# Block 0 of a fused attention and SwiGLU kernel: the norm ahead of the weights' rounding, v from a second queue, and block 1's loads held back

## The chip, the cores and the metric

The kernel runs on one core of a Trainium2 chip. A core has a matrix engine (TensorE, PE in the profile, with its weight loads shown apart as PEld), a vector engine (VectorE, DVE), a scalar engine (ScalarE, ACT), GpSimd (POOL) and SyncE (SP), which here only issues transfers. Each engine carries out its instructions in the order in which they stand in its queue; a wait of one instruction holds all behind it. Transfers are carried out by 16 DMA engines, whichever engine issued them.

The metric is the device time of one launch in microseconds. Before the change the median of four runs is 1042.65 us (1041.47 to 1042.95).

## The reference: what is computed

There are 8 sequences of 576 tokens with 8 heads of width 64, and a feed-forward block over the 4608 tokens.

```
kv  = k^T v                              per sequence and head, 64 x 64
o   = q kv                               per token and head
x   = o / sqrt(mean(o*o) + 1e-6) * g     the norm, over the 64 columns of a head
g   = x @ w_gate ;  val = x @ w_val      4608 x 512  by  512 x 1536
out = (silu(g) * val) @ w_out            4608 x 1536 by 1536 x 512
```

All is float32. The weights come as float64 and are read as pairs of 32-bit words, from which the kernel makes float32 values on the chip ("rounding" below).

## The kernel before

The 4608 tokens are worked in nine blocks of 512 (`NB = 9`). A block's x is 512 tokens by 512 columns. Blocks 1 to 8 use products of the Strassen and Winograd kind (seven products for eight, in classes `Up`, `Inner` and `Down`). Block 0 is different: its up projection is plain (`plain_up`, `plain_end`), because in this stretch the weights arrive and are still being rounded.

**Attention of a block** (class `Att`). `load_kv` and `load_q` issue the loads from SP (L228, L267). `kv` multiplies k and v (L285) into two PSUM tiles, which ACT copies and DVE adds (L291, L292). `turn_q` transposes q on PE (L306) and copies the result to SBUF, on ACT (L308) or on DVE (L310). `product` multiplies by kv (L326), ACT squares the result (L337) and DVE sums the squares (L338). `root` is a chain of eleven small DVE instructions (L344 to L356). `scale` applies the root (two multiplications through the helper of L113). `turn_x` transposes the normed x on PE (L373), and ACT copies it with the gain (L374). Each of these works on half a block (two of four token tiles); `half` is product, root and scale of one half.

**Rounding of a weight piece** (class `Words`). A piece is 128 x 512 values, 512 KB as float64 words. It is loaded by SP (L135) into one of four buffers of the pool `ld`, which the q tiles and later k and v use too. `round_to` makes two ACT instructions (L144, L146) and four DVE instructions (L147, L152, L153, L157) of it. There are 36 pieces: 12 of w_gate and w_val in turn (`g0, v0, g1, v1, ...`), then 12 of w_out. `weights(upto)` rounds pieces up to a number, and before each one issues loads up to four pieces ahead.

**Block 0 in program order.** q of half 0, k and v, q of half 1 are loaded; `weights(1)` loads four pieces and rounds one; `first` does the attention up to the transposed x of half 0; `weights(2)`; `plain_up` for f = 0 and half 0 of the tokens; `second` does root, scale and turn of half 1; then, for each of the twelve f, `weights(2 * (f + 2))` and `plain_up` (L953: four matmuls with the gate, four with the value weights; ACT's silu, L958; DVE's product, L113, which writes h). For f = 0 and 1 the two halves of the tokens are done separately. Then come the w_out pieces' rest, sums for the down projection, block 1's loads, and `plain_end`. A scheduler of the framework sets the order on each engine; it can move instructions past each other where nothing forbids it. `tc.issue_after(ins)` puts the instructions of its block behind `ins` in the order of the engine that `ins` runs on, without a wait of other engines.

Block 1's k and v of the first heads go into a tile of their own (`xi`), its q into tiles of the pool `t`, and the k and v of the other heads into `ld`.

Of the kernel before, what the change touches and what calls it, by code (L numbers as in the profile page):

```python
# [12 lines left out]
ACT = mybir.ActivationFunctionType  # L13
# [5 lines left out]
def kernel(  # L19
# [41 lines left out]
    nc = tc.nc  # L61
# [11 lines left out]
    NP = NF // 2  # L73
# [20 lines left out]
    a_psum = pool("a_psum", 1, space=PS)  # L94
    b_psum = pool("b_psum", 3, space=PS)
# [23 lines left out]
    class Words:  # L119
# [12 lines left out]
        def __init__(self, src, shape):  # L132
            self.raw = ld_pool.tile([P, LD], U32, name="ld")[:, 0 : 2 * BLK]
            dst = self.raw.rearrange("p (a b) -> p a b", a=shape[0])
            nc.sync.dma_start(out=dst, in_=src)  # L135
            self.shape = shape

        def round_to(self, dst):
# [30 lines left out]
    words = {}  # L169

    def load_w(name, j):
        src = wviews[name][1]
        if name == "o":
            words[name, j] = Words(src[:, j : j + 1, :], (1,))
        else:
            words[name, j] = Words(src[:, :, 2 * P * j : 2 * P * (j + 1)], (NS,))
# [8 lines left out]
    class Att:  # L185
# [29 lines left out]
        def load_kv(self, g):  # L215


            if self.n == B:
                return
            for i, (views, src) in enumerate(((self.k, k), (self.v, v))):  # L220
                tile_ = self.place_kv(g, i)
                for e in range(2):
                    j, s0 = 2 * g + e, 0
                    for r in range(2):
                        m = KT - (r != e)
                        at = 2 * D * (KT - r) * e
                        t = tile_[r * D : (r + 1) * D, at : at + 2 * D * m].rearrange("p (h x) -> p h x", h=2)
                        nc.sync.dma_start(  # L228
                            out=t,
                            in_=src[self.n, 2 * j : 2 * j + 2, s0 : s0 + m * D].rearrange("h (p t) d -> p h (t d)", t=m),  # L230
                        )
                        views[j, r] = t.rearrange("p h (t d) -> p h t d", t=m)
                        s0 += m * D
# [60 lines left out]
        def turn_q(self, i, pools=None):  # L294

            if i == 0:
                self.qt = ring().rearrange("p j (t c) -> p t j c", t=T)
            if self.n >= TURNED:
                to = self.qt[:, :, 2 * i : 2 * i + 2].rearrange("p t j c -> p j t c")
                nc.vector.transpose(out=to.rearrange("p j t c -> p (j t c)"), in_=self.q[i])  # L300
                return
            for t in (2 * i, 2 * i + 1):
                pool = pools[t % 2] if pools else m_psum
                ps = pool.tile([P, NS, P], F32, name=pool.name[0])
                for j in range(NS):
                    nc.tensor.transpose(ps[:, j], self.q[t][:, j], ident)  # L306
                if t % 2 or self.n == 1 or self.n > DEEP:
                    nc.scalar.copy(out=self.qt[:, t], in_=ps)  # L308
                else:
                    nc.vector.tensor_copy(out=self.qt[:, t], in_=ps)  # L310

        def product(self, i, pools=None):

            pools = pools or (m_psum, m_psum)
            self.ps[i] = [pool.tile([P, 2, NS, D], F32, name=pool.name[0]) for pool in pools]
            for t in range(2):  # L320
                for j in range(NS):
                    for b, _, p0, p1 in self.parts(2 * i + t):
                        for p in range(p0, p1, D):
                            for u in range(2):
                                rows = slice(u * D, (u + 1) * D)
                                nc.tensor.matmul(  # L326
                                    self.ps[i][u][p : p + D, t, j, :],
                                    lhsT=self.qt[rows, 2 * i + t, j, p : p + D], rhs=kvs[b % 3][rows, j, :],
                                    start=True, stop=True,
                                )  # L330
            if self.z is None or 0 < self.n < TURNED:
                self.z = st_pool.tile([P, 2, 2, 2, NS], F32, name="z")
            if i == 0:
                self.sq = ring().rearrange("p f (t j d) -> p f t j d", t=2, j=NS)
            for u in range(2):
                sq = self.sq[:, 2 * i + u]
                nc.scalar.activation(out=sq, in_=self.ps[i][u], func=ACT.Square)  # L337
                nc.vector.tensor_reduce(out=self.z[:, i, u], in_=sq, axis=mybir.AxisListType.X, op=OP.add)  # L338

        def root(self, i, k=1):  # L340
# [24 lines left out]
        def turn_x(self, i):  # L365
            if i == 0:
                self.x = x_pool.tile([P, 7, 2, HB], F32, name="x")
            xt = self.xts[:, i].rearrange("p t j u d -> p t j (u d)")
            for j in range(0, NS, 2):
                ps = m_psum.tile([P, 2, 2, P], F32, name="m")  # L370
                for e in range(2):
                    for t in range(2):
                        nc.tensor.transpose(ps[:, e, t], xt[:, t, j + e], ident)  # L373
                nc.scalar.activation(  # L374
                    out=self.x[:, 2 * i + j // 2], in_=ps.rearrange("p e t c -> p e (t c)"), func=ACT.Copy, scale=gain
                )

# [49 lines left out]
        def first(self):  # L427
            self.turn_q(0, (b_psum, c_psum))
            for g in range(2):
                self.kv(g)  # L430
            self.half(0)
            self.turn_q(1, (b_psum, c_psum))
            self.product(1, (b_psum, a_psum))
            self.turn_x(0)
            return self.scaled

        def second(self):
            self.root(1)
# [46 lines left out]
    DEEP = 2  # L485
# [482 lines left out]

    pieces = [(x, j) for j in range(NF) for x in "gv"] + [("o", j) for j in range(NF)]
    loaded = rounded = 0  # L970

    def weights(upto):
        nonlocal loaded, rounded
        while rounded < min(upto, len(pieces)):
            while loaded < min(rounded + 4, len(pieces)):
                load_w(*pieces[loaded])
                loaded += 1
            round_w(*pieces[rounded])
            rounded += 1

# [8 lines left out]
    for g in range(2):  # L989
        blocks[0].load_kv(g)  # L990
    blocks[0].load_q(1)
    weights(1)
    scaled = blocks[0].first()

    for n in range(NB):
        ffn = Ffn(n, blocks[n])
        nxt = blocks[n + 1] if n + 1 < NB else None
        if n == 0:

            with tc.issue_after(scaled.ins):  # L1000
                weights(2)
            ffn.plain_up(0, (0,))
            scaled = blocks[0].second()
            for f in range(NF):
                with tc.issue_after(scaled.ins):
                    weights(2 * (f + 2))
                if f == 1:
                    ffn.plain_up(1, (0,))
                    ffn.plain_up(0, (1,))
                ffn.plain_up(f, (1,)) if f == 1 else ffn.plain_up(f) if f else None  # L1010
            weights(len(pieces))
            pairs = wo.rearrange("p (j e) d -> p e j d", e=2)
            t2(pairs[:, 0, :, HD:DM], pairs[:, 1, :, HD:DM], pairs[:, 0, :, 0:HD])
            nxt.room = x_pool.tile([P, 3, 7, P], F32, name="xi").rearrange("p a b c -> p (a b c)")
            for i in range(2):
                nxt.load_kv(i)
            for i in range(2):
                nxt.load_q(i)
            ffn.plain_end()
            for g in range(2):  # L1020
                nxt.kv(g)
        else:

            def third():
                nxt.kv(0)
                nxt.load_kv(1)

            def two_thirds():
                nxt.kv(1)
                if nxt.n < TURNED:  # L1030
                    for i in range(2):
                        nxt.load_q(i)

            ffn.up({4: third, 8: two_thirds} if nxt else {})
        if nxt:
            nxt.turn()
        if n + 2 < NB:
            blocks[n + 2].load_kv(0)
        if TURNED - 2 <= n < NB - 2:
            ffn.loads = blocks[n + 2].load_q  # L1040
            if n >= DEEP:
                for i in range(2):
                    ffn.loads(i)
        ffn.down(nxt)
        if n == 0:

            with tc.issue_after(nxt.halves[0].ins):
                for j in range(NP):
                    t2(wv[j][:, 0:2], wv[j][:, 2:4], wg[j][:, 0:2])
# [31 lines left out]
```

## Time and profile before

| what | value |
|---|---|
| median of the runs | 1042.65 us |
| the profiled execution's own time | 1042.89 us |
| its span | 1041.1 us |
| first matmul of block 0's up projection (L953) | 33.05 us |
| start of f = 1 in it | 39.37 us |
| end of it (start of block 1's L285) | 118.40 us |
| DMA engines' busy share, 2 to 14 us | 0.97 |

Times in the profile are microseconds from the span's start. A row of the timeline gives start, length, engine, line, operation and shapes, and in brackets the idle time of the engine before it and what ended it. The chain that ended last is followed back from the end of the program: at each step it names what released an instruction. The granted clock is the share of full speed that the chip let TensorE run at. In the profile each matmul of 32-bit numbers appears as two instructions, so that the four matmuls of a line are shown as x8.

The rest of the profile is shown in the prediction.

### The profile page before, as it was taken

What the parts mean: (1) busy time and instruction counts of PE and PEld (TensorE: products, weight loads), DVE (VectorE), ACT (ScalarE), POOL (GpSimd) and SP (SyncE); (2) the same over time, 40 slices, a digit from 0 to 9 for tenths busy, and PEclk for the clock granted to TensorE, in tenths of its full rate; (3) what the DMA queues carried; (4) which work ended last, traced back from release to release, by engine and by line L of the source; (5) the groups of instructions that cost most, each with busy time, mean ns of one, the idle gap of its engine ahead of it and who ended that gap; (6) DMA issues with size and microseconds to landing.
All of it is one profiled execution on the core that took longest, in us unless ns stands there. A gap on an engine that the chain in (4) does not pass through costs nothing.

```text
span 1041.1 us, 21533 instructions
## 1 busy us (share of the span) xinstructions
PE 1014.8 (97%) x8588; PEld 911.1 (88%) x8588; DVE 703.1 (68%) x1203; ACT 230.9 (22%) x356; POOL 369.1 (35%) x280
## 2 busy tenths in 40 slices
PE   5899999999999999999999999999999999999998
PEld 4644688788899989998999899988999899989997
DVE  1999596889655756666666756683668566856661
ACT  1666211122212121111121121211222121212110
POOL 0000433445024631563056305550355126512670
PEclk9899999999999999999999999999999999999999
DMA  8797303766467546764677377826862666166611
GB/s 232 217 275 245 115 1 105 195 181 162 111 192 233 149 88 201 249 170 70 197 242 198 55 203 230 223 44 169 249 194 58 156 207 191 30 152 209 192 31 41
DMA packets 255043, 168.15 MB, mean 162 GB/s; under 512 B 124640, under 2 KB 230240, under 8 KB 254944
## 3 DMA queue, kind: packets, MB, share of 16 engines
q1 hardware_dynamic: 229536, 163.63, 56.0%
q10 hardware_dynamic: 25344, 3.15, 1.9%
q8 instruction: 68, 1.11, 0.4%
q14 instruction: 31, 0.25, 0.1%
q0 software_dynamic: 64, 0.00, 0.0%
HBM read 138.02 MB, written 22.41 MB: 154 GB/s over the span
## 4 chain that ended last, share of the span: by engine, by line
PE 91%; DVE 4%; DMA 1%; SPq 1%; issue 1%; POOL 0%; ACT 0%; DVEq 0%; POOLq 0%; ACTq 0%
PE b L659 25%; PE b L510 20%; PE c L659 12%; PE c L510 10%; PE a L659 6%; PE a L510 5%; PE b L953 4%; PE c L953 4%; PE m L285 2%; PE m L326 1%; SPq L228 1%; DMA ld<-in_moe_w_gate_dram 1%; DVE xi L112 1%; DVE r L112 1%; PE m L373 1%
## 5 line engine op out<-in xcount | busy, mean ns | idle before, releaser
L111 POOL TENSOR_TENSOR r<-r 128x256 f32<-128x256 f32 (+1 forms) x105 | 110.8, 1061 | 308.8 <-DVE r L111 234.5
L111 DVE TENSOR_TENSOR r<-b,r 128x512 f32<-128x512 f32 (+1 forms) x273 | 161.9, 605 | 63.7 <-PE b L659 59.2
L112 POOL TENSOR_TENSOR t<-wo 128x512 f32<-128x512 f32 x81 | 115.6, 1452 | 197.6 <-DVE wo L111 109.2
L111 DVE TENSOR_TENSOR r<-c,r 128x512 f32<-128x512 f32 (+1 forms) x179 | 108.3, 617 | 89.5 <-PE c L659 49.3
L659 PE MATMUL b<-x,t 128*128 128x128 f32 x1092 | 151.0, 275 | 0.0
L659 PEld LDWEIGHTS b<-x,t 128*128 128x128 f32 x1092 | 136.5, 192 | 0.6
L111 DVE TENSOR_TENSOR r<-a,r 128x512 f32<-128x512 f32 (+1 forms) x99 | 62.4, 630 | 110.2 <-PE a L510 65.9
L113 POOL TENSOR_TENSOR h<-r 128x1024 f32<-128x1024 f32 (+1 forms) x40 | 81.5, 2052 | 87.5 <-DVE r L111 73.8
L659 PE MATMUL c<-xi,t 128*128 128x128 f32 x840 | 112.2, 275 | 0.3 <-DVE xi L111 0.3
L659 PEld LDWEIGHTS c<-xi,t 128*128 128x128 f32 x840 | 102.8, 192 | 0.4 <-DVE xi L111 0.4
L510 PE MATMUL b<-wo,h 128*128 128x256 f32 x432 | 99.4, 382 | 0.1
L510 PE MATMUL b<-t,h 128*128 128x256 f32 x432 | 96.9, 381 | 0.0
L510 PEld LDWEIGHTS b<-t,h 128*128 128x128 f32 x432 | 81.3, 190 | 11.3 <-issue 0.2
L510 PEld LDWEIGHTS b<-wo,h 128*128 128x128 f32 x432 | 79.9, 190 | 12.7 <-DVE h L113 2.5
L673 ACT COPY r<-b 128x512 f32<-128x512 f32 x63 | 36.9, 585 | 212.7 <-PE b L659 212.7
L659 PE MATMUL b<-xi,t 128*128 128x128 f32 x588 | 79.7, 276 | 0.0
L659 PEld LDWEIGHTS b<-xi,t 128*128 128x128 f32 x588 | 72.4, 192 | 0.0
L659 PE MATMUL b<-x,wg 128*128 128x128 f32 x336 | 52.7, 279 | 0.2 <-DVE x L112 0.2
L659 PE MATMUL b<-x,wv 128*128 128x128 f32 x336 | 51.3, 275 | 0.0
L510 PE MATMUL c<-t,s 128*128 128x256 f32 x216 | 48.3, 380 | 0.0
L510 PE MATMUL a<-wo,h 128*128 128x256 f32 x216 | 48.3, 379 | 0.0
L510 PE MATMUL c<-wo,h 128*128 128x256 f32 x216 | 48.1, 379 | 0.0
(131 smaller groups left out, 1590.1 us busy)
## 6 DMA issues: line engine op xcount, KB each, us to landing
t<-w SPq DMA_DIRECT2D x336, 256.0 KB, 3.4
out_dram<-r SPq DMA_DIRECT2D x17, 512.0 KB, 3.1
ld<-in_moe_w_gate_dram SPq DMA_DIRECT2D x12, 512.0 KB, 5.0
ld<-in_moe_w_val_dram SPq DMA_DIRECT2D x12, 512.0 KB, 4.9
ld<-in_moe_w_out_dram SPq DMA_DIRECT2D x12, 512.0 KB, 4.7
w<-t SPq DMA_DIRECT2D x18, 256.0 KB, 2.5
w<-xi SPq DMA_DIRECT2D x12, 384.0 KB, 3.0
ld<-in_k_dram SPq DMA_DIRECT2D x26, 160.0 KB, 3.7
```

What stands on the lines that cost most here:

```text
L111: add = lambda e, o, a, b: e.tensor_tensor(out=o, in0=a, in1=b, op=OP.add)
L112: sub = lambda e, o, a, b: e.tensor_tensor(out=o, in0=a, in1=b, op=OP.subtract)
L113: mul = lambda e, o, a, b: e.tensor_tensor(out=o, in0=a, in1=b, op=OP.mult)
L228: nc.sync.dma_start(out=t, in_=src[self.n, 2 * j : 2 * j + 2, s0 : s0 + m * D].rearrange("h (p t) d -> p h (t d)", t=m),)
L285: nc.tensor.matmul(self.kv_ps[r][u * D : (u + 1) * D, j, :], lhsT=self.k[j, r][:, u, c, :], rhs=self.v[j, r][:, u, c, :], start=(c == 0), ...
L326: nc.tensor.matmul(self.ps[i][u][p : p + D, t, j, :], lhsT=self.qt[rows, 2 * i + t, j, p : p + D], rhs=kvs[b % 3][rows, j, :], start=True, ...
L373: nc.tensor.transpose(ps[:, e, t], xt[:, t, j + e], ident)
L510: nc.tensor.matmul(banks[e][:, e], lhsT=lhsT, rhs=rhs, start=first and i == 0 and (e == 0 or banks[0] is not banks[1]), stop=i == self.ste ...
L659: nc.tensor.matmul(ps[:, i, f], lhsT=self.weight(o, p, f), rhs=self.operand(o, p), start=first and (i, f) == (0, 0), stop=True, skip_group ...
L673: nc.scalar.copy(out=dst, in_=ps)
L953: nc.tensor.matmul(t, lhsT=w[f // 2][:, i, P * (f % 2) : P * (f % 2 + 1)], rhs=x[:, i, of], start=(i == 0), stop=(i == NS - 1),)
```

## The change

There are five edits.

1. `load_kv` issues block 0's v (eight transfers) from ScalarE's queue instead of SP's.
2. Loading and rounding of weights are split: `load_weights(4)` issues the first four loads, and nothing is rounded before `first`. The first two pieces are rounded behind the last square of half 0 (on ACT) and behind the scale of half 0 (on DVE). From f = 1 on, rounding also stands behind the last copy of x on ACT.
3. In `first`, `product` of half 1 stands inside `issue_after(self.scaled.ins)`: on DVE its sums come behind the scale of half 0.
4. `turn_q` copies on DVE only the first of the four tiles, in every block; before, it was every other tile in blocks 0 and 2 and none in block 1.
5. The thirteen transfers of block 1's q and of its k and v into `xi`, and those of its other k and v, stand on SP's queue behind the load of the 30th of the 36 pieces.

```diff
@@ class Words
-            nc.sync.dma_start(out=dst, in_=src)
+            self.sent = nc.sync.dma_start(out=dst, in_=src)
@@ load_kv
-                        nc.sync.dma_start(
+                        queue = nc.scalar if self.n == 0 and i else nc.sync
+                        queue.dma_start(
@@ turn_q
-                if t % 2 or self.n == 1 or self.n > DEEP:
+                if t:
                     nc.scalar.copy(out=self.qt[:, t], in_=ps)
                 else:
                     nc.vector.tensor_copy(out=self.qt[:, t], in_=ps)
@@ product
-                nc.scalar.activation(out=sq, in_=self.ps[i][u], func=ACT.Square)
+                self.squared = nc.scalar.activation(out=sq, in_=self.ps[i][u], func=ACT.Square)
@@ turn_x
-                nc.scalar.activation(
+                self.copied = nc.scalar.activation(
@@ first
             self.half(0)
+            squared = self.squared
             self.turn_q(1, (b_psum, c_psum))
-            self.product(1, (b_psum, a_psum))
+            with tc.issue_after(self.scaled.ins):
+                self.product(1, (b_psum, a_psum))
             self.turn_x(0)
-            return self.scaled
+            return squared, self.scaled
@@ weights
+    sent = None
+
+    def load_weights(upto):
+        nonlocal loaded, sent
+        while loaded < min(upto, len(pieces)):
+            load_w(*pieces[loaded])
+            loaded += 1
+            if loaded == len(pieces) - NP:
+                sent = words[pieces[loaded - 1]].sent
+
     def weights(upto):
-        nonlocal loaded, rounded
+        nonlocal rounded
         while rounded < min(upto, len(pieces)):
-            while loaded < min(rounded + 4, len(pieces)):
-                load_w(*pieces[loaded])
-                loaded += 1
+            load_weights(rounded + 4)
             round_w(*pieces[rounded])
             rounded += 1
@@ block 0
-    weights(1)
-    scaled = blocks[0].first()
+    load_weights(4)
+    squared, scaled = blocks[0].first()
...
-            with tc.issue_after(scaled.ins):
+            with tc.issue_after(squared.ins), tc.issue_after(scaled.ins):
                 weights(2)
             ffn.plain_up(0, (0,))
             scaled = blocks[0].second()
             for f in range(NF):
-                with tc.issue_after(scaled.ins):
+                with tc.issue_after(scaled.ins), tc.issue_after(blocks[0].copied.ins) if f else ExitStack():
                     weights(2 * (f + 2))
...
-            for i in range(2):
-                nxt.load_kv(i)
-            for i in range(2):
-                nxt.load_q(i)
+            with tc.issue_after(sent.ins):
+                for i in range(2):
+                    nxt.load_kv(i)
+                for i in range(2):
+                    nxt.load_q(i)
```

## The prediction

> **What bounds the kernel now.** I read the busy shares first, then the chain that ended last over the first 66 us, then the windows with the granted clock, then DVE, ACT and SP in order of time. The page says who is the bound:
>
> ```profile
> PE 1014.8 (97%) x8588; PEld 911.1 (88%) x8588; DVE 703.1 (68%) x1203; ACT 230.9 (22%) x356; POOL 369.1 (35%) x280
> ```
>
> PE is idle 26 us of 1041.1, nearly all of it before block 0's first projection and around 200 to 245 us. The change touches the first of these. The chain there (start, length, what):
>
> ```profile
> 13.14 0.58 SPq L267
> ...
> 13.76 7.51 DMA ld<-in_moe_w_gate_dram
> ...
> 21.29 0.43 DVE r L152
> 21.72 0.61 DVE r L310
> ...
> 22.47 2.04 PE m L326 x64
> 24.51 0.59 ACT r L337
> ...
> 25.12 1.29 DVE z L338 x2
> ...
> 29.75 1.30 DVE r L113 x2
> ...
> 31.09 1.97 PE m L373 x8
> 33.05 3.71 PE b L953 x8
> 36.76 1.74 PE c L953 x8
> 38.50 0.87 PE m L373 x8
> 39.37 1.73 PE b L953 x8
> ```
>
> SP issues the twenty loads of q, k and v one after another until 13.72. Then the first piece of w_gate travels 7.51 us. DVE's first rounding instruction (L152) waits for it, and behind it in DVE's order stands the copy of the turned q (L310) that the product (L326) needs. The product could have started far sooner: block 0's kv was summed at 17.23 (16.81 + 0.42, DVE L111). After it come squares, sums, root and scale, stretched by half 1's sums (L338) and root mixed in. From 33.05 PE never waits until block 0 ends.
>
> The windows give the clock (window, length, PE, PEld, DVE, ACT, POOL busy, granted clock, DMA share, GB/s):
>
> ```profile
> 2.00:14.00 12.00, 5.81 (x94) 4.85 (x97) 0.00 (x0) 0.02 (x1) 0.78 (x2) 1.00 0.97 236
> 29.84:33.25 3.41, 2.16 (x9) 1.84 (x10) 3.40 (x9) 1.19 (x3) 0.00 (x0) 0.50 0.12 29
> 33.25:36.66 3.41, 3.41 (x9) 2.69 (x10) 3.18 (x10) 2.51 (x5) 0.00 (x0) 0.50 0.83 225
> 200.51:203.92 3.41, 1.10 (x6) 0.65 (x4) 3.38 (x10) 1.25 (x3) 0.11 (x1) 1.00 0.42 122
> 203.92:207.33 3.41, 3.41 (x8) 2.72 (x9) 2.90 (x9) 0.34 (x1) 0.85 (x1) 0.50 0.65 183
> ```
>
> The clock changes on a grid of 3.41 us. It halves after PE's gap of 26.16 to 31.09 and returns at 36.66, after a window in which PE was busy throughout. The last two rows show that 1.10 us of work in 3.41 does not keep it up. Before 26.43 the column reads 1.00, but four transposes took 1.08 at 4.04 us against 0.60 at 121.23, so PE starts at half.
>
> **The change, part by part.**
>
> *v from ACT's queue.* Eight of SP's issues (0.65 each, 5.2 us) go to ACT. Both queues feed the same 16 DMA engines, whose share in 2 to 14 us was already 0.97, so bytes decide. The first half of q (0.52 MB) and k, v (8 x 160 + 8 x 128 KB = 2.36 MB) at the 241 GB/s of the fully busy early windows take 12.0 us from 2.0: all there at 14.0. Before, PE's last wait for v ended at 15.35. Gain 1.4; bounds 0 (only the issue time was saved) and 2.4 (231 GB/s at share 0.85 in 10 to 12 us is 272 at a full one, landing at 12.6, less some latency). On ACT, eight issues at no more than 0.89 (the 7.08 us for eight at 377 us) plus the table load of 1.28 end by 9.1; the first work there that matters, the kv copy, comes at about 14.9. So ACT's part costs nothing unless kv were ready before 9.1. SP's later k, q and weights wait for semaphores of v loads as well; eight transfers stay in flight, which at some 150 KB keeps the engines full.
>
> [...] The row of 0.84 to 0.94 shares in 8 to 14 us says that issue did hold it a little, so I keep the 1.4.
>
> *Norm ahead of rounding.* kv is summed at 17.23 - 1.4 = 15.8. PE's new order puts the third q tile's transposes ahead of the product: its load follows k, so 0.26 MB more, 15.1; plus 1.11 of transposes, plus 0.4 for landing: the product at 16.6 instead of 22.47. Bounds 15.9 (kv alone) and 18.5 (the same transposes ended at 17.73 before, plus 0.8).
>
> From the product to the end of half 0's scale, with half 1's instructions gone from between: first reduction 2.65 after the product's start (22.47 to 25.12), two reductions 1.31, eleven small DVE steps (L344 to L356) at 0.21 = 2.31, scale 1.33. Sum 7.6, so scale(0) ends at 24.2; before 31.04.
>
> What now stands behind it: the rounding of g0 and v0 was done or hidden before (wg was ready at 24.70, and wv at 33.07 in time for the second operand). Now DVE, in order, does half 1's two reductions (1.28), then L147, L152, L147, L153, L152, L157 at 0.34 + 0.34 + 0.34 + 0.60 + 0.34 + 0.69 = 2.65. wg is ready at 28.1, so the first projection starts at 28.2 instead of 33.05: 4.9 earlier. wv follows 1.3 later, under the first operand's matmuls. ACT's four rounding instructions (4 x 0.55) follow half 1's squares (about 22.7) and end at 25; x is copied by 26.9. Both are hidden by DVE's chain.
>
> *The clock.* PE works from 21.8 to 28.2 only on eight transposes (1 to 2 us). A window inside holds less than the 1.10 us that did not keep the clock at 200 us. So the projection starts at half clock and gets the full one at the first grid point after a full window: between 31.3 and 35.0, mean 33.2. Its 16 matmuls take 6.92 at half, 3.46 at full: end at 17.6 + U/2 = 34.2 (33.2 to 35.1).
>
> [...]
>
> *What is late next.* DVE's order after scale(1) (about 32.8) is now h (L113), then the rounding of g1; before, g1 was rounded first (37.33 to 38.02, h at 38.59). h waits for the projection's end. So wg for f = 1 is ready 0.09 + 0.34 + 2.65 + 0.05 = 3.13 after it: 37.3 (36.3 to 38.2). PE meanwhile does the transposes and two matmuls of f = 0's second half (0.86). f = 1 began at 39.37 before with those two still to do, so PE gains 39.37 - (37.3 - 0.86) = 2.9; by U alone 2.0 to 3.9.
>
> *Does it last to the end of block 0?* DVE is 0.7 us earlier than before with g1, has one h less to do, and afterwards rounds 2.2 us a piece against 3.4 of PE. It ended with slack:
>
> ```profile
> 118.51 0.69 DVE L113 TENSOR_TENSOR h<-h,c 128x512 f32<-128x512 f32 x1 [5.97 <-PE c L953]
> ```
>
> About 3.5 of the 5.97 remain. So all of the 2.9 is kept if the loads keep up.
>
> *Block 1's k, v, q held.* Eight loads of k, v into xi (8 x 0.65) and five of q (5 x 0.55) leave the stretch of 23 to 58 us, where DVE waited for weights at most 1.1 at a time (hidden: PE had no wait), and go behind the 30th piece, among w_out's last six and after. On SP: last piece at 97, v into xi to 100, k and v into ld to 105, q to 108. Bytes from 97 on: 0.5 + 0.6 + 1.2 + 1.0 = 3.3 MB at 241 GB/s, landing at 111. Needed by kv at 115.5 and q's transposes at 117.9 (118.40 and 120.81 less 2.9). Cost 0, cover 4 to 7 us. Block 2's loads behind them move from 105 to 108 us and are used around 180.
>
> *q copies (L307).* Block 0: t = 2 to ACT, which is idle. Block 1: t = 0 to DVE after kv's sum at 122.70; needed at 127.8. Block 2: t = 2 (0.68) leaves DVE at 244 to 250 us, but PE has work from 244.18 on. Cost 0; bounds -0.7 and +0.7.
>
> **Sum.** Profiled execution: span 1041.1, time 1042.89 (1.79 around it). 1042.89 - 2.9 = 1040.0. It lies 0.24 above the median of 1042.65, and its clock came back late (36.66, where 34.2 to 37.9 was possible), so I put the median at 1039.9.
>
> **Rivals.**
> - *Better:* full clock already at 28.2, because the product's run of 16.6 to 21.8 raises it and the short gaps spare it. Then scale(1) at 32.8 decides, f = 1 starts at 35.9, gain 4.4: 1038.4. For it: the 3.14 busy of 3.41 in 23.02 to 26.43 raised it. Against: the row at 200.51.
> - *Eaten:* k and v land no earlier (share 0.97 before) and half 1's transposes or the late clock cost the rest: f = 1 at 39.2, gain 1.0: 1041.7. For it: the q load's 6.7 us of travel at 13.14.
> - *Slower:* block 1's loads come too late. Place: L285 or L306 at 115 to 118 us. PE is paid for each us after 117.9 at which q lands; above 120.8 the kernel is slower than before. That needs the 3.3 MB to travel at below 139 GB/s, or SP to stand 10 us for an ld slot. For it: SP is in order and its k and v wait for slots that the roundings free (99.05, 102.75 before). Against: rates of 223 GB/s in 100 to 110. Price, q at 124: 1042.65 + 3 = 1045.7.
> - *Nothing happens* is excluded: DVE's first instruction is now the q copy, not L152.
>
> **How the numbers follow.** Forecast 0.60, better 0.15, eaten 0.15, slower 0.10. Measurable is about 0.2% (2.1 us): faster means below 1040.6. The forecast's own range is 1038.4 to 1041.4, four fifths of it below 1040.6: faster 0.48 + 0.15 = 0.63, same 0.12 + 0.15 = 0.27, slower 0.10. The range 1037.8 to 1042.3 takes in better and eaten with their spreads and leaves out slower and the tails.
>
> **What the profile after would show.** The q copy first on DVE and the product before 18; scale(0) ending at 24 to 25; wg's first L157 after the reductions at about 28; the first L953 at 28 at half clock; PE waiting for L157 once more before f = 1 at about 37; the last L953 of block 0 ending near 115.5; no wait of L285 or L306 for a DMA. Wrong would be: the product after 18.5, a PE wait on weights between 45 and 115, or a DMA wait at 115.

## The result, and the profile after

The changed kernel takes 1040.68 us (median of 36 runs, 1038.95 to 1042.31), the kernel before beside it 1042.23 us (54 runs, 1040.79 to 1044.14). The ratio is 0.9984 with a 95% interval of 0.9979 to 0.9989: the change saves 1.55 us. That is faster beyond doubt, but by 0.16%, so it falls short of the 0.2% from which the prediction counts a kernel as faster. The profiled execution took 1040.0 us with a span of 1038.2; against the profiled execution of before (1042.89) that is 2.9 us, nearly twice what the medians show. Both numbers have to be explained.

The busy shares of the changed kernel, in the order PE, PEld, DVE, ACT, POOL:

```profile
PE 1010.4 (97%) x8588; PEld 906.9 (87%) x8588; DVE 702.9 (68%) x1202; ACT 231.5 (22%) x357; POOL 372.2 (36%) x280
```

PE is still the bound. Here is the chain that ended last over the first 66 us, as start, length, what:

```profile
0.75 4.13 DMA h<-in_v_dram
...
4.90 5.53 DMA h<-in_k_dram
...
16.67 0.38 ACT kv L292
...
17.55 1.16 PE m L327 x63
18.71 0.75 issue
19.46 0.28 PE m L327
...
23.48 1.29 DVE r L113 x2
24.77 1.19 DVE z L339 x2
...
27.90 0.61 DVE wg L157
...
28.64 3.75 PE b L956 x8
32.40 0.78 PE c L956 x2
33.18 1.65 issue
34.83 0.42 DVE h L113
35.25 0.34 DVE r L147
...
37.19 0.61 DVE wg L157
...
37.85 1.99 PE b L956 x8
...
47.61 3.43 PE b L956 x8
```

The lines have moved by one or three (L326 is now L327, L953 is L956). The first weight piece is gone from the chain. The product (L327) starts at 17.55 instead of 22.47, the first projection at 28.64 instead of 33.05. Between them stand the squares on ACT (until 20.37) and then DVE alone: a sum, root and scale, the sums of half 1, and the six instructions that round g0. After the projection comes a second stretch of DVE, which the kernel before did not have: h at 34.83 (the "issue" of 1.65 ahead of it is the rest of the value matmuls; in the timeline they end at 34.73), then the rounding of g1. PE waits for that until 37.85. In all, f = 2 starts at 47.45 where it was 49.57. These are its first rows in PE's timeline, before and after:

```profile
49.57 3.60 PE L953 MATMUL b<-x,wg 128*128 128x512 f32 x8
47.45 3.60 PE L956 MATMUL b<-x,wg 128*128 128x512 f32 x8
```

The windows, with the same columns as in the prediction (PE, PEld, DVE, ACT, POOL busy, granted clock, DMA share, GB/s):

```profile
2.00:14.00 12.00, 4.40 (x58) 3.80 (x62) 0.69 (x1) 1.76 (x2) 0.78 (x2) 1.00 1.12 238
19.84:23.26 3.42, 1.79 (x68) 1.35 (x67) 2.73 (x13) 2.62 (x6) 0.00 (x0) 1.00 0.89 285
23.26:26.67 3.41, 1.09 (x8) 0.86 (x8) 3.31 (x8) 2.90 (x6) 0.00 (x0) 1.00 0.06 20
26.67:30.09 3.42, 1.45 (x4) 1.21 (x5) 3.39 (x9) 3.40 (x6) 0.00 (x0) 0.50 0.61 182
30.09:33.50 3.41, 3.41 (x10) 2.69 (x9) 2.71 (x11) 0.61 (x2) 0.00 (x0) 0.50 0.37 125
```

The first row is the early loads: 238 GB/s against 236, at a DMA share of 1.12 against 0.97 (the column reads above 1 here). The next rows are the clock: after a window in which PE was busy for 1.79 us it stays, after one with 1.09 it is halved for two windows.

### The profile page after: what moved, and what is told of

Read it like the earlier page. It is cut to its first block, busy times and chain, and to the rows that moved or that the text cites. A ratio compares the mean times of both kernels' runs of the same rounds, so it can differ in the third digit from the quotient of the medians.

```text
span 1038.2 us, 21544 instructions
## 1 busy us (share of the span) xinstructions
PE 1010.4 (97%) x8588; PEld 906.9 (87%) x8588; DVE 702.9 (68%) x1202; ACT 231.5 (22%) x357; POOL 372.2 (36%) x280
## 3 DMA queue, kind: packets, MB, share of 16 engines
q8 instruction: 68, 1.11, 0.4%
## 4 chain that ended last, share of the span: by engine, by line
PE 90%; DVE 6%; DMA 2%; issue 1%; POOL 0%; ACT 0%; SPq 0%; DVEq 0%; POOLq 0%
PE b L662 25%; PE b L513 19%; PE c L662 12%; PE c L513 9%; PE a L662 6%; PE a L513 5%; PE b L956 4%; PE c L956 4%; PE m L286 2%; PE m L327 1%; DVE r L112 1%; DVE xi L112 1%; DVE r L111 1%; DMA w<-t 1%; DMA h<-in_k_dram 1%
## 5 line engine op out<-in xcount | busy, mean ns | idle before, releaser
L112 POOL TENSOR_TENSOR t<-wo 128x512 f32<-128x512 f32 x81 | 118.6, 1488 | 195.4 <-DVE wo L111 110.2
L113 POOL TENSOR_TENSOR h<-r 128x1024 f32<-128x1024 f32 (+1 forms) x40 | 81.7, 2058 | 87.3 <-DVE r L111 74.1
L956 PE MATMUL b<-x,wg 128*128 128x512 f32 (+1 forms) x112 | 45.8, 552 | 3.8 <-DVE wg L157 3.5
```

Of the source, the lines that this page charges most:

```text
L112: sub = lambda e, o, a, b: e.tensor_tensor(out=o, in0=a, in1=b, op=OP.subtract)
L113: mul = lambda e, o, a, b: e.tensor_tensor(out=o, in0=a, in1=b, op=OP.mult)
L956: nc.tensor.matmul(t, lhsT=w[f // 2][:, i, P * (f % 2) : P * (f % 2 + 1)], rhs=x[:, i, of], start=(i == 0), stop=(i == NS - 1),)
```

## The experiments

The theory, T: the norm ahead of the rounding carries the gain; the half clock at the first projection and the new wait behind h keep it small; v's queue and the hold carry little. The rivals: V, that the second queue for v brings k and v in earlier; H, that the hold carries it, because block 1's loads no longer stand among the weights; B, that the gain is made or lost in block 1, by the clock, and hardly in block 0. The kernels ran in three groups (numbers 1 to 4; 6 to 9 without the repetition of 6; the rest), each with its own runs of before (1042.55, 1042.39 and 1042.46 us). Single runs of one kernel scatter by about 0.75 us (standard deviation; 0.5 to 1.2 in the single kernels), so differences of half a microsecond are read from the traces and not from medians.

**1. v back on SP's queue.**

```diff
-                        queue = nc.scalar if self.n == 0 and i else nc.sync
+                        queue = nc.sync
```

> The changed kernel with one part undone: v is loaded from SP again, everything else stays. Theory A (bytes and their efficiency decide the landing of k and v, and a second queue adds nothing: in the changed kernel's profile the DMA share in 2 to 14 us rose from 0.97 to 1.12 at the same 238 GB/s, and the kv copy came at 16.67 instead of 16.34): the same as the changed kernel within 0.4 us, 1040.3 to 1041.1, kv copy at 16.3 to 16.7. Theory B (the prediction's first step: two queues bring kv 1.4 us earlier): 1.4 us slower, 1042.1, kv copy near 18.

Measured: 1041.24 us, ratio 0.9988 (0.998 to 0.9997). The row of 2 to 14 us in its windows:

```profile
2.00:14.00 12.00, 5.75 (x93) 4.86 (x97) 0.69 (x1) 0.61 (x2) 0.78 (x2) 1.00 0.95 236
```

The rate is the same, and the copy of kv (L292) comes at 16.50, not later than with two queues (16.67). PE has 5.75 us of work in this stretch instead of 4.40: with one queue more of k and v was there to be multiplied by 14 us, although the last of it was there no earlier. The product starts at 17.82 (17.55), f = 2 at 47.41 (47.45). So block 0 does not gain from the second queue.

**2. The changed kernel once more**, to have its scatter.

> The changed kernel itself again, as the measure for the three others of this call: 1040.7 within 0.4 us.

Measured: 1040.88 us, ratio 0.9986 (0.9977 to 0.9994). Product 17.75, f = 2 at 47.65.

**3. No hold.** Block 1's loads are issued as before, without the order behind the 30th piece.

```diff
-            with tc.issue_after(sent.ins):
-                for i in range(2):
-                    nxt.load_kv(i)
-                for i in range(2):
-                    nxt.load_q(i)
+            for i in range(2):
+                nxt.load_kv(i)
+            for i in range(2):
+                nxt.load_q(i)
```

> The changed kernel with one part undone: block 1's q, k and v are no longer held behind the 30th piece. Theory A (they travel under work on either place): the same as the changed kernel within 0.4 us, 1040.3 to 1041.1, and PE without a wait between 45 and 115 us. Theory B (the held loads keep the weights' way free, and that is part of the gain): slower by 0.7 to 1.5 us, 1041.4 to 1042.2, with PE waits for rounded weights after 38 us.

Measured: 1040.17 us, ratio 0.9977 (0.9969 to 0.9986). PE's timeline in it shows what the hold takes away:

```profile
36.66 0.57 PE L286 MATMUL m<-xi 64*64 64x64 f32 x22
37.49 1.99 PE L956 MATMUL b<-x,wg 128*128 128x256 f32 x8 [0.27 <-DVE wg L157]
```

Block 1's first k and v are there at 36.66, so 22 rows of its kv fill PE's wait ahead of f = 1; only 0.27 us of it stays idle, where the changed kernel had 0.77. The down projection of block 0, which stands behind block 1's kv, starts at 119.72 us, in the changed kernel at 120.40, in its repetition at 120.60. Some of this is the clock, which came back at 32.79 here and at 33.50 and 33.71 there. The medians differ by 0.7 us in the same direction (means: 0.66 with a 95% interval of about 0.5). H falls: the hold gains nothing; by these runs it costs some half a microsecond.

**4. The norm ahead alone**: the edits of numbers 1 and 3 together, and `turn_q` copies as before.

```diff
-                if t:
+                if t % 2 or self.n == 1 or self.n > DEEP:
```

> The kernel before with only the norm put ahead of the rounding (v on SP, q copies as before, block 1's loads not held). Theory A (the norm's place is the whole gain): as the changed kernel, 1040.3 to 1041.1. Theory B (queue and hold carry half or more of it): 1041.4 to 1042.2. Under both the first projection starts near 28.6 us, at half clock.

Measured: 1041.27 us, ratio 0.9993 (0.9984 to 1.0002). From PE's timeline:

```profile
29.09 3.70 PE L956 MATMUL b<-x,wg 128*128 128x256 f32 x8 [2.30 <-DVE wg L157]
37.63 1.99 PE L956 MATMUL b<-x,wg 128*128 128x256 f32 x8 [0.27 <-DVE wg L157]
47.23 1.02 PE L956 MATMUL b<-x,wg 128*128 128x512 f32 x2
```

The trace and the time say different things. In the trace the norm alone has the whole gain of block 0: f = 2 at 47.23, as early as with everything, and block 0's down projection at 119.83 (number 3: 119.72). The time is 1.1 us above the kernel without the hold, from which it differs by v's queue and the copies of q, and it does not differ from before with certainty. The loss is behind block 0: from the down projection of block 0 to that of block 1 it takes 126.97 us (119.83 to 246.80), the changed kernel 125.54. In this execution the clock halves at 230.58, in the changed kernel's it does not.

**5. v alone**, in the kernel before:

```diff
-                        nc.sync.dma_start(
+                        queue = nc.scalar if self.n == 0 and i else nc.sync
+                        queue.dma_start(
```

> The kernel before with only v loaded from ACT's queue. Theory A (bytes decide, and the first rounding still stands ahead of the q copies): w_gate's first piece lands within 0.7 us of 20.0 to 21.3, the product starts between 21 and 23 and the time is that of the kernel before within 0.5 us. Rival (the issue time saved on SP counts): the piece is issued 2 us or more earlier, the product starts near 20, and the kernel is 1.0 to 1.5 us faster.

Measured: 1042.13 us, ratio 0.9996 (0.9988 to 1.0005). Its row of the windows, then SP's issues from its timeline:

```profile
2.00:14.00 12.00, 4.46 (x61) 3.86 (x65) 0.00 (x0) 1.28 (x1) 0.78 (x2) 1.00 1.13 238
```

```profile
1.85 9.77 SPq L229 DMA_DIRECT2D h<-in_k_dram  x8
```

The same picture as in the changed kernel: more DMA share, no more bytes. SP's eight issues of k, which before stood at 1.84 to 4.65 and 7.30 to 9.85 with v's between them, now stretch over 9.77 us, because k's loads wait for v's (4.1 us in all up to 14 us). The waits of SP's queue in the changed kernel, up to 14 us (in total, times, longest):

```profile
SPq L229 <- DMA h<-in_v_dram: 4.2, 3, 2.2
```

V falls for this kernel: the copy of kv came at 16.38 (16.34 before), and by itself the second queue changes no time that 11 runs can tell.

**6. The second wait taken away.** On DVE, h of f = 0 (the product of silu and value, L113) is put behind the rounding of g1. Helper `round_to` keeps its last instruction, and `plain_up` hands back the product instead of making it.

```diff
+            if later:
+                return lambda: mul(nc.vector, h, h, ps[1])
@@
-            ffn.plain_up(0, (0,))
+            product = ffn.plain_up(0, (0,), later=True)
@@ behind weights(2 * (f + 2))
+                if f == 0:
+                    with tc.issue_after(made["g", 1].made.ins):
+                        product()
```

> The changed kernel with one order changed: DVE multiplies h of f = 0 (first half of the tokens) behind the rounding of g1 instead of ahead of it, as the kernel before did. Theory A (this order is the second wait of the chain, L957 for L157 at 37.85): wg of f = 1 is ready near 35.9, PE goes on without that wait and f = 2 starts 0.7 to 1.0 us earlier, at 46.4 to 46.8 against 47.45. In the time 0.7 to 1.0 less than the changed kernel, 1039.7 to 1040.2. Rival (PE would stand at half clock or for x then anyway): f = 2 within 0.3 of 47.45, no change in the time.

Measured: 1039.11 us, ratio 0.9971 (0.9961 to 0.9981), more than expected. PE's timeline:

```profile
28.06 3.61 PE L957 MATMUL b<-x,wg 128*128 128x256 f32 x8 [2.11 <-DVE wg L157]
34.61 2.59 PE L957 MATMUL b<-x,wg 128*128 128x256 f32 x10 [0.34 <-ACT x L376]
45.24 1.02 PE L957 MATMUL b<-x,wg 128*128 128x512 f32 x2
```

The wait for L157 ahead of f = 1 is gone: the ten rows at 34.61 run from f = 0's second half into f = 1 without a stop, and f = 2 starts at 45.24. Part of that is no merit of the edit: in this execution the clock was full from 14.32 instead of 16.43, so that kv was copied at 15.93 (in the changed kernel at 16.67 and, repeated, 16.87), and it came back at 31.39 instead of 33.50. The last of k and v landed hardly earlier, at 15.24 instead of 15.33. So it was run again, in the next group; what is said there of k and v landing earlier was the clock.

> The changed kernel with h behind g1's rounding, once more. In its first runs it was faster than the kernel before by 0.29% (1039.1 against 1042.4), which is more than the 0.7 to 1.0 us expected over the changed kernel. If that was the order of h alone (first profile: no wait for L157 left before f = 1, f = 2 at 45.24, of which 0.75 came from k and v landing earlier in that execution): f = 2 at 45.2 to 46.2 and a ratio of 0.9968 to 0.9982 to the kernel before. Rival (a lucky set of runs): a ratio of 0.9983 or above, as the changed kernel's.

Measured: 1039.64 us, ratio 0.9973 (0.9963 to 0.9983). Here the clock came back only at 33.99, f = 2 started at 46.83, and still PE did not wait for L157 ahead of f = 1. Against the runs of before in its own group this kernel saves 3.3 and 2.8 us, the changed kernel 1.55 and 1.67. So by the medians the order of h is worth a further 1.1 to 1.7 us, about as much as the whole change, and this version beats both kernels of the case. The trace shows only half of that: with the clock back at about the same time, f = 2 lies 0.6 and 0.8 us ahead of the changed kernel's (47.45 and 47.65), as theory A expected. Where the rest comes from is not shown.

**7. No half clock.** Unread matmuls of `ident` with a loaded tile are added in `first`, five ahead of `turn_x(0)` and three behind it. The rounding of g1 is kept behind h, so that the order on DVE is the changed kernel's.

```diff
+            self.idle(5)
             self.turn_x(0)
+            self.idle(3)
@@
+        def idle(self, count):
+            ps = c_psum.tile([P, BLK], F32, name="c")
+            for _ in range(count):
+                nc.tensor.matmul(ps, lhsT=ident, rhs=self.room[:, 0], start=True, stop=True)
```

> The changed kernel with work added that nobody reads: eight more matmuls of 128x512 on PE (4 x 2 x 0.86 us at full clock) in its idle stretches between the product of half 1 and the first projection, and the rounding of g1 still behind h. Theory A (the half clock of the first projection is PE's own idleness, and costs about 1.3 us net): the granted clock stays 1.00 from 17 to 45 us, the first projection's sixteen rows take 3.5 instead of 6.2 us, and f = 2 starts 1.0 to 1.7 us earlier: 45.8 to 46.5. The time 1039.0 to 1039.8. [...]

Measured: 1040.12 us, ratio 0.9981 (0.9972 to 0.999). Two rows of its windows, over the first projection:

```profile
26.80:30.22 3.42, 3.42 (x12) 1.91 (x11) 3.35 (x10) 3.40 (x6) 0.00 (x0) 1.00 0.66 189
30.22:33.63 3.41, 3.22 (x18) 2.56 (x17) 3.06 (x12) 0.80 (x2) 0.00 (x0) 1.00 0.34 118
```

The clock stays at 1.00, and the projection's sixteen rows take 3.6 us (29.43 to 33.05) instead of 6.1. It starts 0.8 us later than in the changed kernel, behind the last unread matmuls. f = 2 starts at 45.96, 1.5 earlier. So the half clock of the projection goes with PE's own idleness ahead of it: the granted clock was 0.50 over it in the changed kernel and is 1.00 here with the gaps filled, and 1.5 us at f = 2 is its price. The medians, each against its own before, show 0.6 to 0.7 us of it. In this execution the clock halved at 200.88 instead, and from block 0's down projection to block 1's it took 126.35 us, 0.8 more than the changed kernel.

**8. Everything that looked good at once**: the order of 6, the matmuls of 7, v on SP, no hold.

> Four things together: the norm ahead of the rounding as in the changed kernel, v from SP, block 1's loads not held, h behind g1's rounding, and the added matmuls that keep the clock. Theory A: the two waits are separate, so f = 2 starts near 45.5 to 46.2, and the time is 1038.6 to 1039.4. Rival (scale of half 1 at 33 us is the next wait and takes most of it): f = 2 at 46.3 or later, 1039.4 to 1040.2.

Measured: 1041.08 us, ratio 0.9988 (0.9979 to 0.9997). This missed. f = 2 starts at 46.16, earlier than in the changed kernel by 1.3, but no earlier than with 7 alone, and the time is worse than that of 6 by 2 us (1039.11, same group). The trace does not show why: the profiled execution took 1040.01, a microsecond less than the median of the eleven.

**9. Before once more**, in the same group.

> The kernel before, profiled once more, to see how far its block 0 moves with the grid of the clock: f = 2 at 49.6 in the first profile, where the clock came back at 36.66. If the grid's place decides, f = 2 lies between 48.3 and 49.7 and follows the time of the clock's return; if it does not, within 0.1 of 49.6.

Measured: 1042.17 us, ratio 1.0 (0.9991 to 1.0008). Its trace is a second sample of the base. From its chain:

```profile
13.68 6.26 DMA ld<-in_moe_w_gate_dram
...
21.13 2.05 PE m L326 x64
...
48.93 3.43 PE b L953 x8
```

The first piece of w_gate travelled 6.26 us instead of 7.51, the clock came back at 33.74 instead of 36.66, and f = 2 started at 48.77 instead of 49.57. It did not follow the clock's return in full, because here PE waited once more, for the rounding of v1:

```profile
40.03 1.99 PE L953 MATMUL c<-x,wv 128*128 128x256 f32 x8 [1.04 <-DVE wv L157]
```

So the prediction's "From 33.05 PE never waits until block 0 ends" holds for its own profile and not for every execution. The clock halved in block 1 too, at 231.72, and with 1043.52 us this execution was slower than the first one, in spite of the earlier f = 2.

**10. The late h without the hold, and the late h with four and two unread matmuls**, to see what the parts of number 8 do in pairs.

> As e3_again, and block 1's loads not held. Without the hold part of block 1's kv matmuls (L287, 22 rows, 0.5 us) ran in PE's wait before f = 1. Theory A: with h moved there is no such wait left, so these matmuls only change places: f = 2 0.4 to 0.5 us later than without, block 1's down projection at the same point, the time within 0.4 us of e3_again. Rival (the early loads slow the weights): slower by 0.5 to 1.5.

Measured: 1039.77 us, ratio 0.9978 (0.9968 to 0.9988), the same time as with the hold in that group (1039.64). f = 2 started at 46.88. With h late, PE has no wait for g1 left that block 1's kv could fill; its 22 rows run at 36.34 and only change places.

> As e3_again, with six added matmuls that nobody reads (two fewer than before, because the eight ended at 29.4, 1 us after wg was ready). Theory A (scale of half 1 at about 33 is what PE waits for once the clock is full, as in the run with both): f = 2 at 45.0 to 45.6, a gain of no more than 0.3 to 0.8 over e3_again, 1038.6 to 1039.2. Rival (the two waits add up): f = 2 at 44.5 or earlier, 1038 or less.

Measured: 1039.5 us, ratio 0.9972 (0.9962 to 0.9982). f = 2 at 46.10, outside what was expected. PE's timeline shows why the two gains do not add up:

```profile
30.73 1.89 PE L964 MATMUL c<-x,wv 128*128 128x256 f32 x8
33.62 1.06 PE L375 MATMUL m<-ident,r 128*128 128x128 f32 x8 [1.00 <-DVE r L113]
36.07 1.99 PE L964 MATMUL b<-x,wg 128*128 128x256 f32 x8 [0.35 <-DVE wg L157]
```

With the faster projection PE is done with it at 32.6, and then waits 1.00 us for the scale of half 1 (L113), which DVE reaches at its own pace. That is the bound which the case "better" of the prediction put at 32.8 us, and here it takes the place of the clock and of most of the wait behind h (0.35 us of it is left in the third row).

**What v's queue is worth once the norm is ahead** stays open. Three pairs that differ in it, two of them in other edits as well, all favour ScalarE's queue: by 0.4 us (number 1 against 2), 1.1 us (4 against 3) and 1.6 us (8 against 10's second, across groups). At f = 2 the traces show nothing of it (47.41 against 47.45 and 47.65; 47.23 against 47.09; 46.16 against 46.10). All three profiles with v on SP show a drop of the clock between 200 and 236 us, but so do some with v on ScalarE (numbers 6, 7 and 10's second), so the queue is not shown to be the cause. The granted clock of all the runs points the same way: its mean was 0.997 in 23 of the 58 runs of the changed kernel and numbers 2 and 3, and in 1 of the 22 runs of numbers 1 and 4. What that is worth in time is not shown.

## Why the prediction was right or wrong

The sign and the range held (1040.68 in 1037.8 to 1042.3, 0.8 above the forecast). The size did not: 63 chances in 100 were on more than 0.2%, and it was 0.16%.

**v from ACT's queue: wrong.** This is the step that failed: "The row of 0.84 to 0.94 shares in 8 to 14 us says that issue did hold it a little, so I keep the 1.4." In the traces the last of k and v landed at 15.33 us after 15.31 before (forecast 14.0), and kv was copied at 16.67 after 16.34; v alone was worth 0.33 us with an interval that takes in nothing. The two rows side by side, k and v in the changed kernel's timeline:

```profile
1.85 9.83 SPq L229 DMA_DIRECT2D h<-in_k_dram  x8
0.75 8.46 ACTq L229 DMA_DIRECT2D h<-in_v_dram  x8
```

Issuing from a second engine did not bring the bytes sooner; SP spent 4.2 us of the time waiting for transfers of v. Up to eight transfers of k and v were under way at once, as the prediction said, where it had been up to seven, but each took longer (median 4.8 us against 3.8). The two lines are from the views of k's and v's tile, before and after, over the first 20 us:

```profile
DMA to landing us min/median/max: 2.9/3.8/4.6
DMA to landing us min/median/max: 4.1/4.8/6.0
```

A gap in the DMA share (0.84 to 0.94) had been read as a gap in the issuing. The traces agree with the lower bound of 0 that the prediction gave beside its 1.4 (only the issue time saved): 238 GB/s with two queues, 236 with one.

**The product and the norm: right in kind, 0.4 to 1 late.** Forecast 16.6, 24.2, 28.1 and 28.2 for the product, the end of scale, wg and the projection; measured 17.55, 24.77, 28.51 and 28.64. The step from the product to the scale's end took 7.22, not 7.6. That repaid part of v's 1.4. The sum had both reductions behind the last square; here the first of them ran under it:

```profile
18.77 0.60 ACT L338 ACTIVATE r<-m 128x512 f32<-128x512 f32 x1 [0.83 <-PE m L327]
19.40 0.69 DVE L339 TENSOR_REDUCE z<-r 128x8 f32<-128x512 f32 x1 [1.90 <-ACT r L338]
```

The first square could start that early because 63 of the product's 64 rows took 1.16 us: PE's work from 10.47 to 16.6 was one stretch, and the clock was full from 16.43. The product as a whole was no faster. Its last row came at 19.46, behind 0.75 us for which the profile shows no cause, and ended 2.19 us after the first began (2.04 before).

**The clock: right.** The projection began at half clock and the full one came at 33.50 (forecast 31.3 to 35.0). The window of 23.26 to 26.67 with 1.09 us of work halved it, just as the one at 200 us in before, with 1.10. A window that was a third busy was enough. In the repetition the clock fell one window earlier, at 23.47, after a window with PE busy for 1.76 us. Number 7 shows the other side: with the gaps filled the clock stayed at 1.00, in windows with PE busy for at least 2.50 us.

**What is late next: right.** The wait for g1 behind h was forecast to end at 37.3 and ended at 37.85, because the projection ended at 34.73 and not at 34.2; from there to the end of the wait it took 3.12, forecast 3.13. Number 6 shows that it was this order: with h behind g1 the wait is gone. One small term was missing: in the chain the first eight rows behind this wait took 1.99 (at 37.85), where eight rows in a running stretch of before took 1.73 (at 39.37). With it the forecast for f = 2, 49.57 - 2.9 = 46.67, is off by 0.55 + 0.26 = 0.81; measured was 47.45, 0.78 off. So in these two profiles block 0 gained 2.12 and not 2.9, near the lower end of 2.0 to 3.9.

**The end of block 0: right.** The gain lasted. DVE's last h in the changed kernel's timeline:

```profile
116.39 0.69 DVE L113 TENSOR_TENSOR h<-h,c 128x512 f32<-128x512 f32 x1 [2.84 <-PE c L956]
```

2.84 us of idle time were left (forecast 3.5). Block 1's kv started at 116.21 (118.33 before, 2.12 less) and no matmul there waited for a DMA.

**The hold: the cost was not 0.** No load came late, as said, but the cover was smaller than the forecast 4 to 7 us: the last q was issued by 112.8 (forecast 108) and landed at 117.78 (forecast 111), 0.8 us ahead of the first transposes of block 1's q (118.59). What the prediction missed is that loads which come early had a use: PE's new wait could have been filled with block 1's kv (number 3, half a microsecond).

**The sum: right in the profile, wrong in the medians.** The two profiled executions differ by 2.9 us, as forecast, but not for the forecast reason. 2.15 come from block 0 (its down projection starts at 122.55 and 120.40). The other 0.7 go with the clock in block 1: to block 1's down projection it is 126.25 us in before, whose clock halved at 203.92, and 125.54 in after, where it did not. The median is another matter: the profiled execution of before lies 0.66 above the median of its runs, that of after 0.68 below, and these two make up the whole difference of 2.9 and 1.55. The prediction's own step was: "It lies 0.24 above the median of 1042.65, and its clock came back late [...], so I put the median at 1039.9." That stood for a saving of 2.75 us, and it was 1.55. A second profile of before shows that the start of f = 2 varies by 0.8 in one and the same kernel (49.57 and 48.77). Taken over both, before starts f = 2 at 49.2, after (47.45 and 47.65) at 47.55: 1.6 us. So the base of the forecast was at the slow end in block 0, and the forecast took its whole distance as gain. That 1.6 is also what the medians differ by is no proof: the same four executions differ by another 1.05 us in block 1 and by 2.8 in all. What the 1.55 of the medians is made of is therefore not shown run by run. Of the rivals of the experiments B is right in this much: 0.7 us of the difference between the first two profiles, and 1.4 of that between the second two, go with the clock in block 1. What block 0 gains, 2.15 and 1.12 in the two pairs, is T's.

**The rivals.** "Eaten" had the right first half (k and v no earlier), and its 1041.7 lay 1.0 too high. "Better" was shut out by the clock, as argued: it was granted at 0.50 from 26.67 to 33.50. "Slower" did not occur. The measured time lies between the forecast and "eaten".

## What to carry to other kernels

Here, with the DMA engines at a share of 0.97, a second issuing queue brought no more bytes (238 GB/s against 236) and the last of them no sooner (15.33 us against 15.31), so look at the share before a second queue is given; when it is given anyway, see which queue then waits for the other's transfers (here SP for v's, 4.2 us). When work is moved ahead on an engine, read what now stands behind what in its order: here the next wait, h ahead of the next rounding (PE stood until 37.85), was visible in the order, and taking it away too brought, by the medians, about as much again as the whole change. A gain of two or three microseconds in a thousand must be sized from several executions, since the start of one step in one and the same kernel varied by 0.8 us, and the stretch from block 0's down projection to block 1's, in which the clock dropped in ten of fourteen profiles, took 125.5 to 127.0 us.

## What the runs showed of the hardware that was not expected

- Two queues with strided loads of 128 to 160 KB did not bring them sooner. In the nine profiles with v on ScalarE's queue the DMA share of 2 to 14 us was 1.11 to 1.14 at 228 to 247 GB/s, and a transfer took 4.5 to 5.1 us from issue to landing (median); in the five with one queue it was 0.88 to 1.00 at 235 to 239 GB/s, and 3.4 to 3.8 us. The last of k and v landed at 15.1 to 16.0 and at 15.0 to 15.6.
- The windows of 3.41 us with PE busy for 1.09 (the changed kernel, 23.26 to 26.67) and 1.10 us (before, 200.51 to 203.92) were followed by the half clock. No one limit divides the windows of these runs: the clock stayed behind 1.79 (the changed kernel, 19.84 to 23.26), halved behind 1.76 (its repetition, 20.06 to 23.47), and stayed once behind 1.46 (number 9, 201.00 to 204.41). With v on ScalarE's queue PE's kv was done late but in an unbroken stretch, and the full clock came at 14.3 to 16.9 in nine of nine profiles; with v on SP the same work was spread out, and it came at 19.0 to 20.6 in three and at 26.4 and 33.7 in the two of before.
- In ten of the fourteen profiles the clock dropped once more in block 1: over 200 to 236 us its mean was 0.95, in the other four 1.00. These four (the changed kernel, its repetition, numbers 3 and 10's first) took 125.5 to 125.6 us from block 0's down projection to block 1's, the ten with one 126.0 to 127.0. So 0.4 to 1.5 us of a kernel's time went with it. In every profile PE stood still twice in this stretch, for 2.2 to 2.7 us at 197 to 202 and for 1.1 to 2.4 us at 226 to 232. In the ten the window ahead of the drop had PE busy for 0.77 to 1.54 us; in the four the emptiest window there had 1.65 to 1.71. There the grid of 3.41 us shared the longer pause between two windows, and the second pause was 1.7 us long. In number 1, number 4 and the first execution of number 6 the grid shared the longer pause too, but the second one was 1.9 to 2.4 us long, and the clock dropped behind it. So in these profiles the drop went with where the grid fell, which differed from one execution to the next, and with the length of the second pause; what makes that longer was not found.
